# Spreading VectorE's dependent steps in the first pass of an attention and feed-forward kernel

## The chip, the cores and the metric

The kernel runs on one core of a Trainium2 chip. The metric is the device time of one execution in microseconds (us); less is better. The engines are called by the names of the profile: PE (TensorE, matrix products), DVE (VectorE), ACT (ScalarE), POOL (GpSimd) and SP (the engine that issues most DMAs).

## The reference

Chunked attention, then two feed-forward parts. What matters of it:

```python
def _attn_ref(q, k, v):              # 8 batches, 8 heads, 576 positions, 64 wide
    q_c, k_c, v_c = (t.reshape(B, H, 9, 64, 64) for t in (q, k, v))
    scores = 1 / sqrt(64) * matmul(q_c, k_c.transpose(0, 1, 2, 4, 3))
    scores = scores - max(scores, axis=-1, keepdims=True)
    attn = exp(scores)
    attn = attn / (sum(attn, axis=-1, keepdims=True) + 1e-09)
    return matmul(attn, v_c)

x = attn_out.transpose(0, 2, 1, 3).reshape(4608, 512)
h = x @ w_in                         # 512 -> 2048
x = (h * cos(h)) @ w_out             # 2048 -> 512
a, b = x @ w1, x @ w2                # 512 -> 1024 each
out = ((a * b) @ w3) @ w_out2        # 1024 -> 1024 -> 512
```

All of it is f32. The inputs q and k are scaled so that the softmax is not flat.

## The kernel before

**Products.** A product of f32 operands is made of three matmuls on operands split in a high and a low part (hi·hi, hi·lo, lo·hi: lines L111, L112, L113). So each activation and each weight has to be split: ACT or DVE writes the high part, DVE or POOL the low part by a subtraction. For the weights of the first feed-forward part this is done in the kernel: `conv_a`, `conv_b`, `conv_c` (called once each by `conv_tick`, for three different weight tiles in different stages) shift and mask the bits of a weight (L137, L138), add its low half (L144), and split the sum (L189 on ACT, L215 on DVE). From tile 1 on, the `st_...` functions do the same for the weights of later parts (L279, L280, L282, L310), and `sum_make`, `sum_hi`, `sum_lo` make sums of weight blocks for a scheme in which seven products stand for eight ("Seven"; `B11`, `T1` and the like are its operands, made by `x_op` and by L106/L107).

**Tiles.** The 4608 tokens go in 9 tiles of 512. A tile's tokens are four attention blocks of 128 tokens, 36 blocks in all. In the first pass the program goes through tiles 0 to 8, and in each through five groups of hidden columns of the first feed-forward part; a second pass does the other three groups, and then the last stage does the second feed-forward part. While a tile goes through its first four groups, the attention of one block of the next tile runs beside each; the fifth group has no attention, but makes the next tile's operands. Only the first four blocks (0 to 3) have nothing to run beside: they stand in front of tile 0.

**A block's attention** has these steps (the letters are those of the order below): A, scores (PE, L401), their maximum (DVE, L416 for blocks 0 to 3, L421 later) and its subtraction (DVE, L418 or L422); B, exp (ACT, L428); E, the sum (DVE, L433), + 1e-9 (L434), reciprocal (L436) and product (L437); C, four transposes (PE, L444) and a copy to SBUF (ACT, L447); D, the values (PE, L459), the scores of the next block (PE, L401) and a copy of the values into `xf` (ACT, L465 for blocks 0 to 3, L469 later).

**A group's work beside it:** the products of its hidden columns (in tiles 2 and up: `1`, `2`, `5`, `3` in the order, with seven products, and DVE's adds `d`, `e`, `d` between them at L549, L559, L561, L568), the range reduction of the cosine's argument (`a`, `c` on ACT at L607, `A`, `C` on DVE at L612), cos (`b`, `d`, ACT L617), the product with the cosine (`B`, `D`, DVE L621), the split of the result g (`s`: ACT L629, POOL L630 from tile 1 on), and the two halves (`x`, `y`) of the group before's product with w_out (`acc<-g,w`).

**The order** is written out by hand. Each engine takes its instructions in the order in which the program issues them, and waits at the first whose input isn't there. For blocks 0 to 3 it is the string `START`, for a tile's groups a string for the kind of tile: `ORDER0` (tile 0), `ORDER1P` (tile 1), `ORDER1` (tiles 2 to 7), and with an E at its end for the fifth group. A letter issues the part named above; `q` is the next step of attention, `v` a `conv_tick`, `x` in `START` a `conv_tick` too, `o` an operand of the seven products, `l`, `m`, `h`, `r` steps of `st_...`, `M`, `H`, `R` of `sum_...`. Buffers of the tile pools and PSUM banks add the waits that reuse needs.

Of the kernel before, what the change touches and what calls it, by code (L numbers as in the profile page):

```python
# [57 lines left out]
def chunk_attention_two_ffn(  # L58
# [42 lines left out]
    def f32(ap):  # L101
        return ap.bitcast(F32)
# [23 lines left out]
    def conv_a(key):  # L126
# [10 lines left out]
        nc.vector.tensor_scalar(m, hi, 3, 0x3FFFFFFF, op0=ALU.logical_shift_left, op1=ALU.bitwise_and)  # L137
        nc.vector.scalar_tensor_tensor(m, hi, 0xC0000000, m, op0=ALU.bitwise_and, op1=ALU.bitwise_or)  # L138
        halfway[key] = m

    def conv_b(key):

        m = halfway[key].bitcast(I32)
        nc.vector.tensor_tensor(out=m, in0=m, in1=raws.pop(key)[:, :, 0].bitcast(I32), op=ALU.add)  # L144
        if key[0] == "in":
            nc.sync.dma_start(out=wr[key[1] // 2][:, key[1] % 2], in_=m.bitcast(F32))
# [48 lines left out]
    def conv_tick():  # L195

        last = None
# [5 lines left out]
        if cat[2] < cat[1]:  # L203
            conv_b(cq[cat[2]])
            cat[2] += 1
        if cat[1] < cat[0]:
            conv_a(cq[cat[1]])
            cat[1] += 1
        if last:
# [4 lines left out]
            else:  # L214
                nc.vector.tensor_tensor(out=t[:, 1], in0=w, in1=f32(t[:, 0]), op=ALU.subtract)  # L215
# [13 lines left out]
    def sum_make():  # L229
# [10 lines left out]
        sp["parts"] = [(W[pair, 1][:, :, 0:256], s1), (w, spare[:, 0]), (new_s4((pair, 3)), s4)]  # L240

# [28 lines left out]

    def st_bits():
# [3 lines left out]
        key = now.pop("low")  # L275
        raw = raws.pop(key)
        lo, hi = raw[:, :, 0], raw[:, :, 1]
        m = wk.tile([P, TT], U32, tag="cw", name="cw", bufs=3)
        nc.vector.tensor_scalar(m, hi, 3, 0x3FFFFFFF, op0=ALU.logical_shift_left, op1=ALU.bitwise_and)  # L279
        nc.vector.scalar_tensor_tensor(m, hi, 0xC0000000, m, op0=ALU.bitwise_and, op1=ALU.bitwise_or)  # L280
# [113 lines left out]
    def att_scores_mm(j, early):  # L394
# [55 lines left out]
    def att_values(j, early):  # L450
# [908 lines left out]
```

## Time and profile before

| | us |
|---|---|
| time, median of 3 runs (lowest, highest) | 1453.41 (1452.62, 1454.89) |
| time of the profiled execution | 1455.09 |
| span of the profiled execution | 1453.3 |
| PE busy in the span | 1419.9 (98%) |
| DVE busy | 1200.6 (83%) |
| ACT busy | 717.5 (49%) |
| POOL busy | 202.2 (14%) |
| mean granted clock of PE | 0.998 of full speed |

"Busy" sums the durations of an engine's instructions. A row of a timeline gives start and duration in us, engine, line of the kernel before, operation, output and input by the program's names, shapes, a count where several equal instructions are put together, and in square brackets the idle time in front of it with what ended that. The waits are the idle times of one engine grouped by the line that waited and the instruction that it waited for.

### The profile page before, as it was taken

The numbers are of one execution on the slowest core, as the hardware profiler recorded it, in microseconds if no ns is written. First come the engines' busy times: TensorE is split into PE (matmuls) and PEld (weight loads), VectorE is DVE, ScalarE is ACT, GpSimd is POOL, SyncE is SP. The second block draws the span as 40 slices with busy tenths as digits, with TensorE's granted clock in tenths as the row PEclk, the third lists the DMA queues.
The fourth block names the chain that finished last, engine by engine and source line by source line (L and its number), as shares of the span: only waits on it lengthen the run. The fifth ranks groups of instructions, "written<-read, shape, count | busy, mean of one in ns | idle before, by whom it ended". The sixth has DMA issues, their size and how long they took to land.

```text
span 1453.3 us, 27397 instructions
## 1 busy us (share of the span) xinstructions
PE 1419.9 (98%) x10572; PEld 1260.6 (87%) x10572; DVE 1200.6 (83%) x1995; ACT 717.5 (49%) x1201; POOL 202.2 (14%) x151
## 2 busy tenths in 40 slices
PE   5899999999999999999999999999999999999998
PEld 5788878888888889888888889998898888889888
DVE  7989899899998987777777888776797888788787
ACT  4877677777777774444445544331132133123122
POOL 0112112222222222222212223020000000000000
PEclk9999999999999999999999999999999999999999
DMA  8866556566664628989899984697565765856643
GB/s 274 259 201 194 212 158 239 178 216 231 197 237 162 224 98 320 364 303 339 306 311 346 366 318 168 231 364 261 217 231 192 266 202 174 326 170 207 232 145 116
DMA packets 152481, 347.31 MB, mean 239 GB/s; under 512 B 15392, under 2 KB 53024, under 8 KB 151200
## 3 DMA queue, kind: packets, MB, share of 16 engines
q1 hardware_dynamic: 151200, 343.47, 68.2%
q0 software_dynamic: 1152, 2.10, 0.8%
q8 instruction: 84, 1.38, 0.4%
q14 instruction: 45, 0.37, 0.1%
HBM read 241.96 MB, written 101.45 MB: 236 GB/s over the span
## 4 chain that ended last, share of the span: by engine, by line
PE 59%; DMA 1%; DVE 1%; POOL 1%; ACT 1%; issue 0%; SPq 0%; POOLq 0%; ACTq 0%
PE ps_hh L111 7%; PE ps_hh L112 7%; PE ps_hh L113 7%; PE acc L112 7%; PE acc L113 7%; PE acc L111 7%; PE ps_aa L111 5%; PE ps_aa L112 5%; PE ps_aa L113 5%; POOL g L630 1%; DMA sd<-spare 0%; DMA raw<-in_w_dram 0%; DMA wfd<-wfo 0%; ACT T L106 0%; DVE x2a L659 0%
## 5 line engine op out<-in xcount | busy, mean ns | idle before, releaser
L630 POOL TENSOR_TENSOR g<-t,g 128x512 fp32r<-128x512 f32 x134 | 187.0, 1416 | 637.0 <-ACT g L629 596.7
L111 PE MATMUL acc<-g,w 128*128 128x512 f32 x576 | 228.1, 396 | 0.0
L112 PE MATMUL acc<-g,w 128*128 128x512 f32 x576 | 227.0, 394 | 0.4
L113 PE MATMUL acc<-g,w 128*128 128x512 f32 x576 | 225.0, 391 | 0.0
L860 ACT ACTIVATE phl<-w 128x512 fp32r<-128x512 f32 x66 | 41.3, 631 | 292.0 <-DVE w L1051 242.1
L113 PE MATMUL ps_hh<-T,w 128*128 128x256 f32 (+1 forms) x616 | 181.8, 295 | 1.7 <-DVE w L215 1.7
L111 PE MATMUL ps_hh<-T,w 128*128 128x256 f32 (+1 forms) x616 | 181.8, 295 | 0.0
L112 PE MATMUL ps_hh<-T,w 128*128 128x256 f32 (+1 forms) x616 | 181.6, 295 | 0.0
L112 PEld LDWEIGHTS acc<-g,w 128*128 128x128 f32 x576 | 108.5, 188 | 23.8 <-POOL g L630 4.0
L113 PEld LDWEIGHTS acc<-g,w 128*128 128x128 f32 x576 | 108.2, 188 | 22.8
L111 PEld LDWEIGHTS acc<-g,w 128*128 128x128 f32 x576 | 108.5, 188 | 19.6
L113 PEld LDWEIGHTS ps_hh<-T,w 128*128 128x128 f32 x616 | 118.2, 192 | 4.8 <-DVE w L215 2.3
L111 PE MATMUL ps_hh<-B,w 128*128 128x256 f32 (+1 forms) x396 | 120.2, 304 | 1.1 <-ACT xf L465 0.5
L111 PEld LDWEIGHTS ps_hh<-T,w 128*128 128x128 f32 x616 | 118.3, 192 | 2.7
L112 PEld LDWEIGHTS ps_hh<-T,w 128*128 128x128 f32 x616 | 118.3, 192 | 2.4
L112 PE MATMUL ps_hh<-B,w 128*128 128x256 f32 (+1 forms) x396 | 116.5, 294 | 0.0
L113 PE MATMUL ps_hh<-B,w 128*128 128x256 f32 (+1 forms) x396 | 116.3, 294 | 0.0
L617 ACT ACTIVATE t<-t,half_pi 128x512 f32<-128x512 f32 x144 | 98.5, 716 | 1.1
L629 ACT ACTIVATE g<-t 128x512 fp32r<-128x512 f32 x144 | 85.4, 628 | 12.3 <-DVE t L621 10.6
L607 ACT ACTIVATE t<-d 128x512 int32<-128x512 f32 x62 | 39.2, 632 | 103.3 <-DVE d L561 99.6
L111 PEld LDWEIGHTS ps_hh<-B,w 128*128 128x128 f32 x396 | 76.5, 193 | 6.6 <-PE acc L113 0.8
L549 DVE TENSOR_TENSOR d<-x,ps_hh 128x512 f32<-128x512 f32 x70 | 47.9, 685 | 40.5 <-ACT g L629 27.2
(304 smaller groups left out, 3775.5 us busy)
## 6 DMA issues: line engine op xcount, KB each, us to landing
w<-sd SPq DMA_DIRECT2D x159, 512.0 KB, 5.6
sd<-raw SPq DMA_DIRECT2D x104, 256.0 KB, 4.3
wset<-twd SPq DMA_DIRECT2D x26, 512.0 KB, 4.0
s<-sd SPq DMA_DIRECT2D x43, 256.0 KB, 5.7
wset<-wfd SPq DMA_DIRECT2D x42, 256.0 KB, 4.4
qk<-in_q_dram SPq DMA_DIRECT2D x36, 256.0 KB, 4.0
qk<-in_k_dram SPq DMA_DIRECT2D x36, 256.0 KB, 4.2
x2a<-x2o SPq DMA_DIRECT2D x36, 256.0 KB, 3.1
```

Source lines behind the costliest of these rows:

```text
L111: nc.tensor.matmul(ps, a[0], b[0], start=first, stop=False)
L112: nc.tensor.matmul(ps, a[0], b[1], start=False, stop=False)
L113: nc.tensor.matmul(ps, a[1], b[0], start=False, stop=last)
L549: nc.vector.tensor_tensor(out=two(self.d), in0=self.x1.unsqueeze(1).to_broadcast([P, 2, 256]), in1=two(p26), op=ALU.add)
L607: nc.scalar.activation(t.bitcast(I32), h, AF.Copy, scale=INV2PI, bias=0.25)
L617: nc.scalar.activation(t, t, AF.Sin, scale=TWO_PI, bias=half_pi)
L629: nc.scalar.activation(hi, r, AF.Copy)
L630: (nc.vector if i < GA else nc.gpsimd).tensor_tensor(out=lo, in0=r, in1=f32(hi), op=ALU.subtract)
L860: nc.scalar.activation(put[kind, f][0], plane(*SRC[kind], f), AF.Copy)
```

## The change

The text of `START` and of the orders changes, and with it the steps that an order can name. The attention's step A is cut in scores and maximum (A) and subtraction (F); step E in sum (E), + 1e-9 (G), reciprocal (I) and product (K). `conv_tick` issues DVE's instructions of its three stages in another order (shift, add, sign, low part; before: add, shift, sign, low part) and can issue attention steps between them. `st_bits` is cut in shift (`t`), sign (`n`) and the rest (`m`); `sum_make` in two parts (`M`, `N`). In `START` the scores of block 3 (`M3`) are issued before the transposes of block 0.

```diff
-START = "A0 A1 B0 x B1 E0 A2 C0 B2 E1 A3 D0 C1 x B3 D1 E2 o o E3 C2 D2 x C3 D3 x o o"
+START = "A0 F0 A1 F1 B0 x B1 E0 A2 M3 G0 I0 F2 K0 C0 B2 E1 A3 G1 I1 F3 K1 D0 C1 B3 x2 D1 o o x3 C2 D2 C3 D3 x o o"
-ORDER0 = "PsvaAqQvqcCqxybBdvDqvq"
+ORDER0 = "PsvaqAqQvqqcCqxybqBqdvDqvq"
-ORDER1P = "PsqMhQqqHaclAxbqCrRBmdyqDL"
+ORDER1P = "PsqMqNhQqqHaclAqtqxbCqnqrRBmdyqDL"
-ORDER1 = "1s2qMh5qqHa3clAxbqCrRmBdyqDL"
+ORDER1 = "1sq2qMNh5qqHa3cqlAqtqxbCnqrRmBdyqDL"
...
-        nc.vector.tensor_scalar(m, hi, 3, 0x3FFFFFFF, op0=ALU.logical_shift_left, op1=ALU.bitwise_and)
-        nc.vector.scalar_tensor_tensor(m, hi, 0xC0000000, m, op0=ALU.bitwise_and, op1=ALU.bitwise_or)
         halfway[key] = m
+        return (lambda: nc.vector.tensor_scalar(m, hi, 3, 0x3FFFFFFF, op0=ALU.logical_shift_left, op1=ALU.bitwise_and),
+                lambda: nc.vector.scalar_tensor_tensor(m, hi, 0xC0000000, m, op0=ALU.bitwise_and, op1=ALU.bitwise_or))
...
-    def conv_tick():
+    def conv_tick(between=()):
...
         if cat[2] < cat[1]:
-            conv_b(cq[cat[2]])
+            add = conv_b(cq[cat[2]])
             cat[2] += 1
         if cat[1] < cat[0]:
-            conv_a(cq[cat[1]])
+            bits = conv_a(cq[cat[1]])
             cat[1] += 1
+        ops = [*bits[:1], *([add] if add else ()), *bits[1:]]
...
-                nc.vector.tensor_tensor(out=t[:, 1], in0=w, in1=f32(t[:, 0]), op=ALU.subtract)
+                ops.append(lambda: nc.vector.tensor_tensor(out=t[:, 1], in0=w, in1=f32(t[:, 0]), op=ALU.subtract))
+        between = list(between)
+        for op in ops:
+            op()
+            if between:
+                between.pop(0)()
+        for op in between:
+            op()
...
+        nc.vector.tensor_tensor(out=s1, in0=a21, in1=a22, op=ALU.add)
+        sp["parts"] = None
+        yield
         nc.vector.tensor_tensor(out=s3, in0=a11, in1=a21, op=ALU.subtract)
-        nc.vector.tensor_tensor(out=s1, in0=a21, in1=a22, op=ALU.add)
         nc.vector.tensor_tensor(out=s2, in0=s1, in1=a11, op=ALU.subtract)
...
+    def att_sum(j, early):
+        sums[j] = sm = small.tile([P, 2 * HP], F32, tag="sm", name="sm")
+        nc.vector.reduce_sum(out=sm, in_=att[j], axis=AX.X)
+
+    def att_guard(j, early):
+        nc.vector.tensor_scalar_add(sums[j], sums[j], 1e-9)
+
+    def att_recip(j, early):
+        sm = sums[j]
+        sums[j] = rc = small.tile([P, 2 * HP], F32, tag="rc", name="rc")
+        nc.vector.reciprocal(rc, sm)
+
     def att_scale(j, early):
-        ex = att[j]
-        sm = small.tile([P, 2 * HP], F32, tag="sm", name="sm")
-        nc.vector.reduce_sum(out=sm, in_=ex, axis=AX.X)
-        nc.vector.tensor_scalar_add(sm, sm, 1e-9)
-        rc = small.tile([P, 2 * HP], F32, tag="rc", name="rc")
-        nc.vector.reciprocal(rc, sm)
+        ex, rc = att[j], sums.pop(j)
         nc.vector.tensor_tensor(
             out=ex, in0=ex, in1=rc.unsqueeze(2).to_broadcast([P, 2 * HP, 64]), op=ALU.mult)
...
-            if tok == "x":
-                conv_tick()
+            if tok[0] == "x":
+                conv_tick([lambda s=s_: att_tok(s + tok[1:], True) for s_ in "EGIK"] if tok[1:] else ())
...
-        steps = [s + str(j) for j in range(4, NJ) for s in "ABECD"]
+        steps = [s + str(j) for j in range(4, NJ) for s in "AFBEGIKCD"]
```

What this makes of VectorE's order is shown at three places. A row is the line, the operation, and output <- inputs with the columns.

First, the blocks in front of tile 0, with the buffers' numbers. `ex_260` belongs to block 1, `sm_312` and `rc_315` (after: `sm_330`, `rc_339`) are its sum and reciprocal; `mx_339` (after: `mx_335`) is block 3's maximum and `ps_s0`, `ps_s1` hold its scores. Before:

```order
L433 TENSOR_REDUCE sm_312<-ex_260 128x8
L434 TENSOR_SCALAR sm_312<-sm_312 128x8
L436 RECIPROCAL rc_315<-sm_312 128x8
L437 TENSOR_TENSOR ex_260<-ex_260,rc_315 128x512
L416 TENSOR_REDUCE mx_339<-ps_s0_318 128x4
L416 TENSOR_REDUCE mx_339<-ps_s1_319 128x4
L418 TENSOR_TENSOR two_301<-ps_s0_318,mx_339 128x4x64
L418 TENSOR_TENSOR two_301<-ps_s1_319,mx_339 128x4x64
```

After, at the same place:

```order
L466 TENSOR_REDUCE sm_330<-ex_260 128x8
L442 TENSOR_REDUCE mx_335<-ps_s0_300 128x4
L442 TENSOR_REDUCE mx_335<-ps_s1_301 128x4
L469 TENSOR_SCALAR sm_330<-sm_330 128x8
L474 RECIPROCAL rc_339<-sm_330 128x8
L451 TENSOR_TENSOR two_297<-ps_s0_300,mx_335 128x4x64
L451 TENSOR_TENSOR two_297<-ps_s1_301,mx_335 128x4x64
L478 TENSOR_TENSOR ex_260<-ex_260,rc_339 128x512
```

Block 1's product (L437, after L478), ahead of block 3's maximum before, now stands behind its maximum and its subtraction.

Second, the end of the same stretch on VectorE: block 3's sum and product, and the two low parts of operands (L107) ahead of them. Before:

```order
L107 TENSOR_TENSOR B11_176<-xf_174,B11_176 128x512
L107 TENSOR_TENSOR B21_177<-xf_174,B21_177 128x512
L433 TENSOR_REDUCE sm_408<-two_301 128x8
L434 TENSOR_SCALAR sm_408<-sm_408 128x8
L436 RECIPROCAL rc_411<-sm_408 128x8
L437 TENSOR_TENSOR two_301<-two_301,rc_411 128x512
L144 ISA cw_371<-raw_196,cw_371 128x1024
L137 TENSOR_SCALAR cw_443<-raw_270 128x512
L138 SCALAR_TENSOR_TENSOR cw_443<-raw_270,cw_443 128x512
L215 TENSOR_TENSOR w_439<-cw_266,w_439 128x512
```

After:

```order
L107 TENSOR_TENSOR B11_176<-xf_174,B11_176 128x512
L107 TENSOR_TENSOR B21_177<-xf_174,B21_177 128x512
L138 TENSOR_SCALAR cw_410<-raw_270 128x512
L466 TENSOR_REDUCE sm_413<-two_297 128x8
L146 ISA cw_370<-raw_196,cw_370 128x1024
L469 TENSOR_SCALAR sm_413<-sm_413 128x8
L139 SCALAR_TENSOR_TENSOR cw_410<-raw_270,cw_410 128x512
L474 RECIPROCAL rc_419<-sm_413 128x8
L220 TENSOR_TENSOR w_408<-cw_266,w_408 128x512
L478 TENSOR_TENSOR two_297<-two_297,rc_419 128x512
```

The four instructions of a weight conversion stood behind block 3's product and now stand between its steps, ahead of the product.

Third, a group of tiles 2 to 7 on VectorE, without buffers' numbers (`ps_at` is the bank of the attention, `ps_hh` the banks of the hidden columns, `t` the cosine's argument, `cw` a weight's bits). Before:

```order
L549 TENSOR_TENSOR d<-x_2503,ps_hh 128x512
L421 TENSOR_REDUCE mx<-ps_at 128x8
L422 TENSOR_TENSOR ex<-ps_at,mx 128x2x4x64
L559 TENSOR_TENSOR e<-d,ps_hh 128x512
L561 TENSOR_TENSOR d<-e,ps_hh 128x256
L433 TENSOR_REDUCE sm<-ex 128x8
L434 TENSOR_SCALAR sm<-sm 128x8
L436 RECIPROCAL rc<-sm 128x8
L437 TENSOR_TENSOR ex<-ex,rc 128x512
L568 TENSOR_TENSOR e<-e,ps_hh 128x512
L612 SCALAR_TENSOR_TENSOR t<-d,t 128x512
```

After:

```order
L444 TENSOR_REDUCE mx<-ps_at 128x8
L594 TENSOR_TENSOR d<-x_2503,ps_hh 128x512
L454 TENSOR_TENSOR ex<-ps_at,mx 128x2x4x64
L604 TENSOR_TENSOR e<-d,ps_hh 128x512
L606 TENSOR_TENSOR d<-e,ps_hh 128x256
L466 TENSOR_REDUCE sm<-ex 128x8
L613 TENSOR_TENSOR e<-e,ps_hh 128x512
L469 TENSOR_SCALAR sm<-sm 128x8
L657 SCALAR_TENSOR_TENSOR t<-d,t 128x512
L474 RECIPROCAL rc<-sm 128x8
L291 TENSOR_SCALAR cw<-raw 128x512
L478 TENSOR_TENSOR ex<-ex,rc 128x512
```

The maximum now stands ahead of the add that frees a bank of the hidden columns (L549, after L594), and between the sum and the product stand a 512-wide add, a step of the cosine and a shift of weight bits. On PE the order is the same but for one place: block 0's transposes stand behind block 3's scores. On SP and POOL nothing moves. On ACT, from tile 1 on, the copy of the transposes (L447, after L488) stands behind the load of the cosine's table and the first cosine, where before it stood ahead of both.

## Rows read from the trace of the kernel before

**Rows 1.** Busy time by stretch: start and end, length, each engine, clock, DMA.

```profile
0.00:100.00 100.00, 77.23 (x909) 68.21 (x910) 86.00 (x165) 71.40 (x120) 7.98 (x14) 0.97 0.85 258
...
200.00:545.00 345.00, 343.21 (x3355) 301.87 (x3355) 310.32 (x546) 262.05 (x416) 79.66 (x57) 1.00 0.58 194
545.00:1454.00 909.00, 903.29 (x5360) 805.27 (x5358) 715.45 (x1131) 310.42 (x547) 95.68 (x67) 1.00 0.73 259
```

**Rows 2.** Waits of PE for VectorE: total us, times, longest.

```profile
PE ps_at L444 <- DVE ex L437: 10.6, 7, 3.7
...
PE ps_hh L113 <- DVE w L215: 1.7, 3, 0.6
PE ps_hh L111 <- DVE d L549: 1.5, 2, 1.4
```

**Rows 3.** Timeline of PE, from the first blocks to the first group.

```profile
15.21 1.13 PE L401 MATMUL ps_s<-qk 64*64 64x64 f32 x32 [1.46 <-DMA qk<-in_k_dram]
...
17.13 1.12 PE L444 MATMUL ps_at<-ident,ex 128*128 128x128 f32 x4
...
28.32 0.58 PE L111 MATMUL ps_hh<-B,w 128*128 128x256 f32 x1 [0.47 <-ACT xf L465]
...
41.10 1.12 PE L444 MATMUL ps_at<-ident,ex 128*128 128x128 f32 x4 [3.67 <-DVE ex L437]
```

**Rows 4.** Timeline of VectorE in the first blocks.

```profile
16.39 0.76 DVE L416 TENSOR_REDUCE mx<-ps_s 128x4 f32<-128x256 f32 x2 [0.78 <-PE ps_s L401]
...
21.55 1.29 DVE L107 TENSOR_TENSOR B<-xf,B 128x512 fp32r<-128x512 f32 x2 [0.32 <-ACT B L106]
...
23.91 0.69 DVE L437 TENSOR_TENSOR two<-two,rc 128x512 f32<-128x512 f32 x1
...
25.13 0.42 DVE L137 TENSOR_SCALAR cw<-raw 128x512 uint32<-128x512 uint32 x1
```

**Rows 5.** Tile 1, a group with weight sums: VectorE, then PE.

```profile
119.95 0.69 DVE L437 TENSOR_TENSOR ex<-ex,rc 128x512 f32<-128x512 f32 x1
...
122.19 0.60 PE L444 MATMUL ps_at<-ident,ex 128*128 128x128 f32 x4
```

**Rows 6.** Tile 2, timeline of PE where an add comes late.

```profile
183.01 0.39 PE L111 MATMUL ps_hh<-B,s 128*128 128x256 f32 x1 [1.39 <-DVE d L549]
```

**Rows 7.** Tile 3, VectorE in a group that is not the tile's first.

```profile
268.99 0.69 DVE L549 TENSOR_TENSOR d<-x,ps_hh 128x512 f32<-128x512 f32 x1 [0.29 <-PE ps_hh L113]
...
270.32 0.69 DVE L422 TENSOR_TENSOR ex<-ps_at,mx 128x512 f32<-128x512 f32 x1
...
271.98 0.68 DVE L433 TENSOR_REDUCE sm<-ex 128x8 f32<-128x512 f32 x1
272.69 0.17 DVE L434 TENSOR_SCALAR sm<-sm 128x8 f32<-128x8 f32 x1
272.89 0.20 DVE L436 RECIPROCAL rc<-sm 128x8 f32<-128x8 f32 x1
273.13 0.69 DVE L437 TENSOR_TENSOR ex<-ex,rc 128x512 f32<-128x512 f32 x1
273.74 0.68 DVE L568 TENSOR_TENSOR e<-e,ps_hh 128x512 f32<-128x512 f32 x1
```

**Rows 8.** The same group: ACT, then PE.

```profile
271.20 0.63 ACT L428 ACTIVATE ex<-ex 128x512 f32<-128x512 f32 x1
...
276.21 1.28 ACT L617 ACT_TABLE_LOAD   x1
...
274.48 0.60 PE L444 MATMUL ps_at<-ident,ex 128*128 128x128 f32 x4
...
277.77 0.70 PE L459 MATMUL ps_at<-pt,vt 64*64 64x64 f32 x32
```

**Rows 9.** The first group of a later tile: VectorE, then PE.

```profile
292.62 0.68 DVE L549 TENSOR_TENSOR d<-x,ps_hh 128x512 f32<-128x512 f32 x1
...
293.36 0.39 PE L111 MATMUL ps_hh<-B,s 128*128 128x256 f32 x1
```

More of the change, by code (lines that the diff above doesn't have):

```diff
@@ L193, in chunk_attention_two_ffn @@
     cq, cat = [], [0, 0, 0, 0]
-    def conv_tick():
-        last = None
+    def conv_tick(between=()):
+        last, add, bits = None, None, ()
         if cat[3] < cat[2]:
@@ L269, in st_low, with st_shift, st_sign @@
             nc.scalar.activation(lo.bitcast(I32), lo, AF.Copy, scale=2.0 ** -29)
+    def st_shift():
+        if "low" in now:
+            now["m"] = m = wk.tile([P, TT], U32, tag="cw", name="cw", bufs=3)
+            hi = raws[now["low"]][:, :, 1]
+            nc.vector.tensor_scalar(m, hi, 3, 0x3FFFFFFF, op0=ALU.logical_shift_left, op1=ALU.bitwise_and)
+    def st_sign():
+        if "low" in now:
+            m = now["m"]
+            hi = raws[now["low"]][:, :, 1]
+            nc.vector.scalar_tensor_tensor(m, hi, 0xC0000000, m, op0=ALU.bitwise_and, op1=ALU.bitwise_or)
     def st_bits():
@@ L274, in st_bits @@
             return
-        key = now.pop("low")
+        key, m = now.pop("low"), now.pop("m")
         raw = raws.pop(key)
[L277 to L280, printed above, removed]
+        lo = raw[:, :, 0]
         mi = m.bitcast(I32)
@@ L407, in att_scores @@
             att_scores_mm(j, early)
+        while qk_at[0] < min(NJ, j + 2 + early):
+            load_qk(qk_at[0])
         ps = scores.pop(j)
@@ L416, in att_scores, with att_below @@
                 nc.vector.reduce_max(out=mx[:, c], in_=ps[c], axis=AX.X)
+        else:
+            nc.vector.reduce_max(out=mx, in_=ps, axis=AX.X)
+        scores[j] = ps, mx, ex
+    def att_below(j, early):
+        ps, mx, ex = scores.pop(j)
+        if early:
             for c in range(2):
@@ L473, in att_tok @@
     def att_tok(step, early):
-        (att_scores, att_softmax, att_scale, att_transpose, att_values)["ABECD".index(step[0])](int(step[1:]), early)
+        part = {"A": att_scores, "F": att_below, "B": att_softmax, "E": att_sum, "G": att_guard, "I": att_recip,
+                "K": att_scale, "C": att_transpose, "D": att_values, "M": att_scores_mm}[step[0]]
+        part(int(step[1:]), early)
     OPS = ("B11", "B21", "T2", "T1", "T3", "B22", "T4")
@@ L1130, in chunk_attention_two_ffn @@
         n_sums = 0
+        sums2 = []
         fq = 0
@@ L1189, in chunk_attention_two_ffn @@
                         n_sums += 1
-                elif op == "M":
-                    if loaded and i > GA + loaded[0][0]:
-                        sum_make()
+                elif op in "MN":
+                    if op == "N" and sums2:
+                        next(sums2.pop())
+                    elif op == "M" and loaded and i > GA + loaded[0][0]:
+                        sums2.append(sum_make())
+                        next(sums2[0])
                 elif op in "HR":
@@ L1197, in chunk_attention_two_ffn @@
                     st_low()
+                elif op == "t":
+                    st_shift()
+                elif op == "n":
+                    st_sign()
                 elif op == "m":
@@ L1215, in chunk_attention_two_ffn @@
                     if i < iA and nth < 4:
-                        att_tok(steps[20 * n + 5 * nth + n_q], False)
+                        att_tok(steps[36 * n + 9 * nth + n_q], False)
                     elif i >= iB + FOLD and fq < 4 * FB2:
```

24 lines of the change are left out of this document (13 added, 11 removed).

## The prediction

> **What bounds the kernel now.** The busy time by stretch comes first [rows 1]. After 545 us PE is busy for 903 of 909 us, and from 200 to 545 us, where the later tiles of the first pass run, for 343.2 of 345. VectorE is busy for 310 of those 345 us, but that alone is no cost: PE sets the pace, and what VectorE does counts only where PE waits for it. Only the first 100 us are open: PE 77 of 100. So the second view is PE's waits [rows 2]. For VectorE they come to little: 10.6 us at the transposes (seven waits, for the softmax product L437), 1.7 at weights (L215, three waits), 1.5 at the add L549. Of the 10.6, two waits of about 3.7 stand in the first 42 us, the second in tile 0's first group [rows 3]. That is all that a quicker VectorE can give back, some 14 us, and any step of VectorE that comes later than its slack is paid in full, since PE has nothing else to do. So the change is judged by one question at each place: when do the transposes' input (the product), the freed bank (the add), and the low part of a weight come, against the moment at which PE gets there.
>
> **What an opened pair is worth.** In a group of tile 3 [rows 7] the sum L433 starts at 271.98 and takes 0.68; the guard that needs it starts at 272.69, 0.03 after its end. Guard, reciprocal and product follow each 0.03 to 0.04 after the one before. But the add L568, which doesn't need the product in front of it, starts at 273.74, 0.08 before that product ends (273.13 + 0.69). So a step behind its own input pays 0.11 us more than one behind another's, and a 512-wide step costs 0.61 in a stream. A group opens about six such pairs (maximum to subtraction, sum to guard, guard to reciprocal, reciprocal to product, shift to sign, sign to add): 0.7 us of VectorE. For the guard and the reciprocal behind another instruction there is no row. Bounds: their present spacing, 0.20 and 0.24, and their durations less 0.08, 0.09 and 0.12 [rows 7]. I take 0.10 and 0.12, since the 0.08 is what the one independent pair there shows. A shift of weight bits, 0.42 long [rows 4], costs 0.34 by the same step.
>
> The Trainium skill, "VectorE: DVE Perf Modes", section "The DRAIN you can't avoid", speaks against this: an instruction starts when the pipe is empty, and eight copies with a semaphore after each took as long as eight with one after the last. By that an opened pair gives nothing. The 0.03 after against 0.08 before the end [rows 7] does not agree with it.
>
> **The blocks in front of tile 0: +3.4 us.** The two places in the order show it. Block 3's scores start at 15.21, when their keys arrive [rows 3], and nothing in the order of the loads moves, so issuing them earlier brings them no earlier. Before, block 1's product was done ahead of block 3's maximum at 16.39 [rows 4], and its transposes ran at 17.13 [rows 3]. Now that product stands behind that maximum and its subtraction: 16.39 + 0.67 (two halves of the maximum) + 0.2 (guard, reciprocal, adjacent) + 0.7 (two halves of the subtraction, taken as long as the maximum's) + 0.69 (itself) is about 18.7. Block 1's transposes start at about 18.75, 1.6 late; its values, their copy and the low parts L107 behind them go from 21.55 [rows 4] to about 23.2. Behind L107 (1.2) VectorE now has ahead of block 3's product: shift 0.34, sum 0.61, add 0.61, guard 0.10, sign 0.61, reciprocal 0.12, low part 0.61, together 4.2. It starts at about 27.4 instead of 23.91 [rows 4], 3.45 late. From that product to the first matmul of group 0 it is 28.32 - 23.91 = 4.41 (transposes, copy, values, copy; all in a row), so that matmul goes to about 31.8. Nothing later gives this back, since the rest runs at PE's pace. Block 0's transposes, now behind block 3's scores, cost nothing by themselves: its values stood behind those scores before too. Ends: +1.8, if only the second part is paid (the 4.2 less the old 2.4 ahead of the product), and +4.6, with small steps at their present spacing and ACT's copies late as well.
>
> **Tile 0: -1.35.** In its first group the transposes at 41.10 wait 3.67 for the product [rows 3], and VectorE is on that path. The product now has the cosine's product ahead of it, +0.61, less two or three opened pairs, 0.26: +0.35 (0 to +0.6). In the other groups VectorE sheds about 0.9 a group (softmax and four conversions), so the three waits for weights, 0.6 at most [rows 2], should go: -1.7 (-1.7 to 0).
>
> **Tile 1: +0.6.** In three groups with weight sums the product ends at 120.64 and the transposes start at 122.19 [rows 5]: slack 1.55. Now two steps of the cosine (0.6 each) and a shift (0.34) stand ahead of it, 1.54, less what the pairs give. I take 0.2 each, 0 to 0.5.
>
> **Tile 2: -0.8.** VectorE is behind for two groups; PE waits 1.39 for the add [rows 6], and most of the 3.2 us of waits at transposes outside the two long ones [rows 2] is here. Two groups' savings, 1.4, less 0.6 for the maximum that now stands ahead of the add. Ends: -2.7 (nearly all of it) and +0.5.
>
> **Tiles 3 to 7, the first group of each: +4.0.** The third place in the order shows why. The add L549 frees a bank; it starts at 292.62 straight behind VectorE's earlier work and ends at 293.30; PE's next product starts at 293.36 [rows 9]. The maximum now stands ahead of the add: 0.6, with no slack. The products behind it come late too; I add 0.2 at the transposes: 0.8 in each of five groups. Ends: 0.2 and 0.9 a group (1.0 to 4.5), the low one if VectorE gets there earlier.
>
> **Tiles 3 to 7, the other fifteen groups: +2.5.** Here VectorE waits 0.29 before the add [rows 7], so the maximum fits in front, and the subtraction moves from 270.32 to about 269.8. The exp can follow by some 0.25 only: it ends a stream of ACT (271.20, 0.19 after its input's end at 271.01 [rows 7, 8]). The sum then starts at about 271.55 instead of 271.98. Behind it, up to the product: sum 0.61, add 0.61, guard 0.10, cosine step 0.61, reciprocal 0.12, shift 0.34, that is 2.4 where it was 1.15. The product ends at about 274.65 instead of 273.82; the transposes start at 274.48 [rows 8]. So 0.15 to 0.2 is lost, in groups with an extra sum or shift 0.25: about 2.5 in all, ends 0 and 0.35 each (0 to 5.2).
>
> ACT's copy of the transposes now stands behind the table load of 1.28 and one cosine. The values that read it start at 277.77, 2.7 us after the transposes end at 275.08 [rows 8], and the load starts earlier, because the add L568 that releases the step ahead of it comes at 272.2 instead of 273.74 [rows 7]. I take nothing. Without that lead the copy would end at about 276.2 + 1.3 + 0.6 + 0.6 = 278.7, 0.9 late in each group.
>
> The second pass and the last stage keep PE's order and its pace [rows 1]: nothing.
>
> **Sum.** 3.4 + 0.35 - 1.7 + 0.6 - 0.8 + 4.0 + 2.5 = +8.35. It is made against the profiled execution (1455.09, of which 1453.3 is span); the median of the three runs is 1.7 lower. I put the difference on the median: 1453.41 + 8.4 = 1461.8.
>
> **Rivals.**
>
> Slower, but at the start only. VectorE arrives 0.6 or more ahead in each tile's first group and 0.2 ahead in the others, so the groups of tiles 3 to 7 lose nothing. For it: 0.7 saved a group. Against it: in [rows 9] the add is at the end of VectorE's queue. 3.4 + 0.35 - 1.7 + 0.6 - 0.8 is +1.85: 1455.3.
>
> Faster. VectorE's saved time reaches PE: the 1.7, the 3.2 at transposes and the 1.4 at the add go, -6.3, and the start loses its lower end, +1.8: -4.5, 1448.9. Its place is tiles 0 to 2; it decides if the keys of block 3 come some 1.4 us before 15.21, so that block 1's product isn't late, and if VectorE keeps 0.6 of slack in tiles 3 to 7. For it: these waits are real. Against it: the loads keep their order.
>
> An opened pair gives nothing, as a mechanism of this kernel: the small steps keep 0.20, 0.24 and 0.45. Then the start is +3.75, the product in fifteen groups 0.33 later (+5), the 1.7 stays and tile 2 gains nothing: about +16, 1469. The add at 273.74 [rows 7] speaks against it. The rule of "VectorE: DVE Perf Modes" named above would have it so.
>
> **How the numbers follow.** Chances: my sum 0.57, the start only 0.23, faster 0.14, pairs worth nothing 0.06. A measurement of this kernel tells about 0.2% from no change, 2.9 us: 1450.5 to 1456.3. The start-only case lies mostly within it (0.17), the low edge of my sum too (0.03). Faster 0.14, same 0.20, slower 0.66. The lower ends together make about -1.6, the upper ones +17, but they won't all fall on one side; the range leaves out the faster case and the worthless pairs: 1453.5 to 1467.5.
>
> **What would show it.** In the trace after: the first matmul of group 0 near 31.8, behind a product of block 3 at 27.4; in each tile's first group PE waiting some 0.6 for the add (now L594); waits of 0.1 to 0.4 at the transposes for the product (L478) in tiles 3 to 7; no waits at the weights (L220); small steps 0.09 to 0.13 apart from the next. I am wrong if the first matmul starts before 30, if the add in a first group starts no later against PE than before, or if the table load of the cosine makes the values wait for their copy.

## The result, and the profile after

The changed kernel takes 1464.51 us (median of four runs, 1463.69 to 1465.79) against 1453.01 (four runs of the kernel before). The ratio is 1.0077, with a 95% interval of 1.0063 to 1.0091: slower by about 11.2 us. The prediction was 1461.8, in a range of 1453.5 to 1467.5.

Busy time by stretch, as in [rows 1] (start and end, length, then PE, PE's weight loads, VectorE, ACT, POOL, PE's clock, DMA share, GB/s), of the changed kernel:

```profile
0.00:100.00 100.00, 74.19 (x895) 65.32 (x896) 79.37 (x160) 69.00 (x116) 7.79 (x14) 0.97 0.81 247
...
200.00:545.00 345.00, 338.67 (x3330) 296.20 (x3329) 292.42 (x538) 260.69 (x412) 78.26 (x57) 1.00 0.57 192
```

VectorE's busy time from 200 to 545 us fell from 310 to 292 us. Part of that is work that now falls behind 545 us. Between the same two events, the first transposes of blocks 15 and 35, it is 273.7 us (485 instructions) before and 262.3 (484) after: the spread steps do save some 11 us of its time. PE's busy time fell too, from 343.2 to 338.7, since it now waits more. PE's waits of the changed kernel, as in [rows 2]:

```profile
PE ps_at L485 <- DVE ex L478: 10.6, 9, 4.0
PE ps_hh L111 <- DVE d L594: 3.7, 5, 0.7
PE ps_v L500 <- ACT two L488: 3.1, 2, 2.4
PE ps_at L500 <- ACT pt L488: 2.7, 4, 0.7
...
PE ps_hh L113 <- DVE w L220: 1.5, 3, 0.5
```

The transposes wait as long as before (10.6), at other places; the add waits 3.7 instead of 1.5, in five places; the weights still wait 1.5.

Where the time went is best read from one event that every kernel has, the first transpose of each attention block on PE. The table gives its start in each profile and how much later it is than in the kernel before; negative is earlier. Blocks 4 to 7 run in tile 0, 8 to 11 in tile 1, and so on, and blocks 12, 16, 20, 24, 28 and 32 in the first group of a tile.

| block | before, us | after, us | later by | softmax and start of before, only the weights spread (experiment 5): later by |
|---|---|---|---|---|
| 3 | 24.66 | 27.86 | 3.20 | -0.12 |
| 4 | 41.10 | 44.47 | 3.37 | -0.92 |
| 8 | 109.20 | 112.40 | 3.20 | -1.97 |
| 11 | 148.16 | 152.76 | 4.60 | -1.97 |
| 12 | 173.18 | 178.42 | 5.24 | -2.09 |
| 13 | 188.79 | 192.82 | 4.03 | -3.44 |
| 14 | 201.21 | 206.80 | 5.59 | -3.56 |
| 15 | 213.48 | 219.18 | 5.70 | -3.57 |
| 16 | 236.81 | 243.22 | 6.41 | -3.58 |
| 35 | 516.57 | 527.55 | 10.98 | -5.39 |

So the start costs about 3.2, tile 0 nothing, tile 1 1.4, block 14 a step of 1.56 that no wait there explains (below), each tile's first group about 0.7, and the rest a tenth or two at a time; tile 2 gives 0.57 back (block 11 to 13). The last column is the experiment that came out faster than both; it stands here to be read beside the others.

In the first blocks (timeline of PE, changed kernel; compare [rows 3]):

```profile
14.57 1.25 PE L427 MATMUL ps_s<-qk 64*64 64x64 f32 x32 [5.46 <-DMA qk<-in_k_dram]
15.76 1.11 PE L485 MATMUL ps_at<-ident,ex 128*128 128x128 f32 x4
17.56 1.14 PE L500 MATMUL ps_v<-ex,vt 64*64 64x64 f32 x32 [0.69 <-ACT ex L488]
18.62 1.11 PE L485 MATMUL ps_at<-ident,ex 128*128 128x128 f32 x4
...
31.36 0.58 PE L111 MATMUL ps_hh<-B,w 128*128 128x256 f32 x1 [0.47 <-ACT xf L506]
```

and on VectorE there (compare [rows 4]; the second line is block 1's product, the last block 3's):

```profile
15.86 0.76 DVE L442 TENSOR_REDUCE mx<-ps_s 128x4 f32<-128x256 f32 x2 [2.26 <-PE ps_s L427]
...
17.46 0.68 DVE L478 TENSOR_TENSOR ex<-ex,rc 128x512 f32<-128x512 f32 x1
...
27.12 0.68 DVE L478 TENSOR_TENSOR two<-two,rc 128x512 f32<-128x512 f32 x1
```

Block 3's product starts at 27.12 (27.4 was forecast; 23.91 before), the first matmul at 31.36 (31.8; 28.32 before). PE waited 5.46 us for block 3's keys, which now stand ahead of block 0's transposes.

A tile's first group, VectorE and then PE (compare [rows 9]):

```profile
299.34 0.68 DVE L444 TENSOR_REDUCE mx<-ps_at 128x8 f32<-128x512 f32 x1
299.94 0.68 DVE L594 TENSOR_TENSOR d<-x,ps_hh 128x512 f32<-128x512 f32 x1
...
300.67 0.39 PE L111 MATMUL ps_hh<-B,s 128*128 128x256 f32 x1 [0.74 <-DVE d L594]
```

The maximum takes the place that the add had, and PE waits 0.74. This is there in the first group of each of tiles 3 to 7.

A later group, VectorE, then PE (compare [rows 7] and the last but one of [rows 8]):

```profile
278.15 0.68 DVE L466 TENSOR_REDUCE sm<-ex 128x8 f32<-128x512 f32 x1
278.74 0.68 DVE L613 TENSOR_TENSOR e<-e,ps_hh 128x512 f32<-128x512 f32 x1
279.34 0.16 DVE L469 TENSOR_SCALAR sm<-sm 128x8 f32<-128x8 f32 x1
279.41 0.68 DVE L657 SCALAR_TENSOR_TENSOR t<-d,t 128x512 f32<-128x512 f32 x1
280.01 0.19 DVE L474 RECIPROCAL rc<-sm 128x8 f32<-128x8 f32 x1
280.13 0.37 DVE L291 TENSOR_SCALAR cw<-raw 128x512 uint32<-128x512 uint32 x1
280.42 0.68 DVE L478 TENSOR_TENSOR ex<-ex,rc 128x512 f32<-128x512 f32 x1
...
281.15 0.66 PE L485 MATMUL ps_at<-ident,ex 128*128 128x128 f32 x4
```

From the sum's start to the product's start it is 2.27 us, where it was 1.15. Each step starts about 0.08 before the one in front of it ends, the guard (the step that adds 1e-9) costs 0.07, the reciprocal 0.12: VectorE loses no time between steps, and the product comes later, as other work stands in its chain.

### The profile page after: what moved, and what is told of

Its sections match the earlier page's. It is cut to its first block, busy times and chain, and to the rows that moved or that the text cites. A ratio compares the mean times of both kernels' runs of the same rounds, so it can differ in the third digit from the quotient of the medians.

```text
span 1463.4 us, 27436 instructions
## 1 busy us (share of the span) xinstructions
PE 1422.0 (97%) x10572; PEld 1259.6 (86%) x10572; DVE 1175.3 (80%) x1995; ACT 716.8 (49%) x1201; POOL 202.2 (14%) x151
## 3 DMA queue, kind: packets, MB, share of 16 engines
q1 hardware_dynamic: 151200, 343.47, 67.7%
## 4 chain that ended last, share of the span: by engine, by line
PE 60%; POOL 1%; ACT 1%; DVE 1%; issue 0%; POOLq 0%; ACTq 0%
PE ps_hh L111 8%; PE ps_hh L112 8%; PE ps_hh L113 8%; PE acc L112 7%; PE acc L113 7%; PE acc L111 7%; PE ps_aa L111 6%; PE ps_aa L112 6%; PE ps_aa L113 6%; POOL g L675 1%; ACT T L106 0%; DVE T L107 0%; ACT g L674 0%; ACT t L662 0%; ACT B L106 0%
## 5 line engine op out<-in xcount | busy, mean ns | idle before, releaser
L594 DVE TENSOR_TENSOR d<-x,ps_hh 128x512 f32<-128x512 f32 x70 | 47.9, 684 | 57.0 <-ACT g L674 50.0
```

The lines of the kernel that those rows point to most:

```text
L594: nc.vector.tensor_tensor(out=two(self.d), in0=self.x1.unsqueeze(1).to_broadcast([P, 2, 256]), in1=two(p26), op=ALU.add)
```

## The experiments

All kernels are compared with the kernel before on the same chip. "Lateness" is the number of the table: the start of a block's first transpose against the kernel before.

**1. The start put back.** The order ahead of tile 0 as before, all else as changed.

```diff
-START = "A0 F0 A1 F1 B0 x B1 E0 A2 M3 G0 I0 F2 K0 C0 B2 E1 A3 G1 I1 F3 K1 D0 C1 B3 x2 D1 o o x3 C2 D2 C3 D3 x o o"
+START = "A0 F0 A1 F1 B0 x B1 E0 G0 I0 K0 A2 F2 C0 B2 E1 G1 I1 K1 A3 F3 D0 C1 x B3 D1 E2 G2 I2 K2 o o E3 G3 I3 K3 C2 D2 x C3 D3 x o o"
```

> The changed kernel, with the stretch ahead of tile 0 in the order of before (block 3's scores behind block 0's transposes, each block's sum, guard, reciprocal and product in a row, weights converted behind block 3's product). Theory: that stretch costs what it moves, the trace of after has its first matmul at 31.36 against 28.32, and block 4's transposes 3.4 us late; so the first matmul comes back to about 28.3 and the time falls by about 3.2, to 1461.3. Rival: the wait of 4.05 at the transposes of the first group, which VectorE sets, swallows it, since VectorE then has the conversions still to do: the time falls by less than 1 us, 1464.

Measured: 1461.11 us, before 1454.44, ratio 1.0045 (1.0030 to 1.0060). The first matmul starts at 28.35, and block 4 is 0.82 early where it was 3.37 late: the start's cost is real and is not swallowed. From block 14 to 35 the lateness grows by 5.4 as in the changed kernel. At block 14 the step of 1.56 is missing here.

**2. The maximum behind the add again**, in tiles 2 to 7.

```diff
-ORDER1 = "1sq2qMNh5qqHa3cqlAqtqxbCnqrRmBdyqDL"
+ORDER1 = "1s2qqMNh5qqHa3cqlAqtqxbCnqrRmBdyqDL"
```

> The changed kernel, with the maximum behind the add again in tiles 2 to 7 (maximum and subtraction in a row). Theory: the five waits of 0.74 for the add in the first group of tiles 3 to 7 go, 3.7 us, and 0.1 comes back per group where the subtraction follows its own maximum but has slack: about -3.5, 1461. Rival: VectorE's queue is as late with the add in front, because the maximum only changes places with other work, and the wait moves to the transposes of the same group: less than 1.5 us.

Measured: 1472.97 us, ratio 1.0126 (1.0110 to 1.0141): 8.5 more than the changed kernel's median, 7 by the two ratios. Both expectations fell. PE's waits:

```profile
PE ps_at L485 <- DVE ex L478: 20.5, 28, 4.0
```

The waits for the add are gone, but the transposes now wait for the product in 28 places. Each group of tiles 3 to 7 now adds about 0.6 of lateness, where the changed kernel adds 0.1 in most. So the maximum ahead of the add, which costs the first groups 0.7, pays for a part of what the other moves cost everywhere else: in blocks 16 to 35 the exp starts 1.76 us behind the first add (L594) in the changed kernel and 2.05 here, the sum 2.44 and 2.98 (medians).

**3. Sum to product in a row**, ahead of the last add, with the maximum still ahead; here the transposes also stand behind `b`, as in the changed kernel.

```diff
-ORDER1 = "1sq2qMNh5qqHa3cqlAqtqxbCnqrRmBdyqDL"
+ORDER1 = "1sq2qMNh5qqqqqHa3clAtxbqCnrRmBdyqDL"
```

> The changed kernel, with sum, guard, reciprocal and product in a row ahead of the last add in tiles 2 to 7; the maximum still ahead of the first add. Theory: what stands between the sum and the product makes the transposes late; the waits of 0.74 (three) fall to 0.3 or less, tile 2's 1.56 and 1.95 fall by 0.6 each, and the 0.1 lost in each other group goes: -1.7 for tiles 3 to 7, -1.2 for tile 2, and with the wait of 1.95 shortened the clock of 0.57 behind it is not seen, another -1.5: 1460 to 1461.5. Rival: the transposes wait for the exp on ACT, and the order of what follows it matters little: within 1 us of the changed kernel.

Measured: 1463.36 us, ratio 1.0060 (1.0043 to 1.0076): 1.2 less than the changed kernel's median, 2.5 by the two ratios, so between the rival and the theory. PE's waits:

```profile
PE ps_at L500 <- ACT pt L488: 8.2, 14, 1.0
PE ps_at L485 <- DVE ex L478: 6.2, 6, 4.0
```

The waits at the transposes fell as the theory has it (4.0 of the 6.2 us is the first group), but new ones stand in their place: the values wait for ACT's copy. Four of the 14 places, 2.7 us, are tile 0's and are there before too; the ten others, 5.5 us, are in tiles 2 to 7. The last add is behind the product again, and with it the table load that the copy stands behind.

**4. Only the weights' part**, with the transposes behind `b`.

```diff
+START = "A0 F0 A1 F1 B0 x B1 E0 G0 I0 K0 A2 F2 C0 B2 E1 G1 I1 K1 A3 F3 D0 C1 x B3 D1 E2 G2 I2 K2 o o E3 G3 I3 K3 C2 D2 x C3 D3 x o o"
+ORDER0 = "PsvaAqqQvqcCqqqqxybBdvDqvq"
+ORDER1P = "PsqqMNhQqqqqqHaclAtxbqCnrRBmdyqDL"
+ORDER1 = "1s2qqMNh5qqqqqHa3clAtxbqCnrRmBdyqDL"
```

> Only the weights' part of the change: conversions (shift, add, sign, low part), the bits' steps and the sums spread as in the changed kernel; all of the softmax and the stretch ahead of tile 0 as before. Theory: VectorE has less to do, but PE waits for it no less, since in tile 0 the order that leads to the late weight starts at an exp and a cosine of ACT: 1452 to 1454, within 1 us of before. Rival 1: the weights' order alone costs what after lost outside the first blocks, 6 us or more. Rival 2: it is worth the 1.7 us of waits at weights and more: 1450 or less.

Measured: 1465.61 us, ratio 1.0078 (1.0062 to 1.0093). Taken alone that looks like rival 1. The waits say what it is:

```profile
PE ps_at L500 <- ACT pt L488: 19.0, 28, 1.0
```

Four of the 28, 2.7 us, are tile 0's, as before; the other 24, 0.5 to 1.0 us each, are in tiles 2 to 7. This kernel kept one thing of the softmax's change: ACT's copy of the transposes behind the cosine's table load, where before has it ahead in these tiles (in tile 1 it stands behind the load before too, from 123.33 us behind a load from 121.40, and no wait comes of it). ACT in one group, then PE, then the copy in the kernel before, whose table load follows at 276.21 [rows 8]:

```profile
277.03 0.63 ACT L652 ACTIVATE t<-e 128x512 int32<-128x512 f32 x1 [1.73 <-DVE e L613]
...
278.24 1.28 ACT L662 ACT_TABLE_LOAD   x1
279.54 0.73 ACT L662 ACTIVATE t<-t,half_pi 128x512 f32<-128x512 f32 x1
280.17 0.58 ACT L488 ACTIVATE pt<-ps_at 128x512 f32<-128x512 f32 x1
...
280.80 0.69 PE L500 MATMUL ps_at<-pt,vt 64*64 64x64 f32 x32 [0.54 <-ACT pt L488]
```

```profile
275.61 0.58 ACT L447 ACTIVATE pt<-ps_at 128x512 f32<-128x512 f32 x1
```

The last add is late as before, ACT's step that waits for it (1.73) holds the table load, and the copy ends at 280.75. In the changed kernel that add stands ahead of the product, so the table load starts before the transposes and the copy costs nothing.

**5. The same with the copy ahead of the table load**, as before has it in tiles 2 to 7 (here in tile 1 too).

```diff
-ORDER1P = "PsqqMNhQqqqqqHaclAtxbqCnrRBmdyqDL"
-ORDER1 = "1s2qqMNh5qqqqqHa3clAtxbqCnrRmBdyqDL"
+ORDER1P = "PsqqMNhQqqqqqHaclAtxqbCnrRBmdyqDL"
+ORDER1 = "1s2qqMNh5qqqqqHa3clAtxqbCnrRmBdyqDL"
```

> As the kernel with only the weights' part of the change, but with the copy of the transposes ahead of the cosine's table load on ACT, as before has it (there it stood behind the table load and the first cosine, and PE waited for it at 28 places, 19.0 us in all). Theory: those waits, about 0.7 each in tiles 1 to 7, go; the weights' part alone is then no loss: 1452 to 1454 on a chip where before takes 1453 to 1454. Rival: the copy's waits turn into waits for the product: 1460 or more.

Measured: 1449.89 us, before 1453.57, ratio 0.9972 (0.9962 to 0.9982): faster than both kernels by more than was expected. Busy time and the waits that are left:

```profile
200.00:545.00 345.00, 343.94 (x3369) 303.57 (x3368) 306.57 (x547) 262.13 (x418) 81.25 (x58) 1.00 0.58 196
```

```profile
PE ps_at L485 <- DVE ex L478: 9.8, 4, 4.0
...
PE ps_hh L113 <- DVE w L220: 0.9, 3, 0.4
...
PE ps_hh L111 <- DVE d L594: 0.5, 2, 0.3
```

The gain stands in tile 0 (1.05 from block 4 to 8, with the weights' waits down to 0.9), in tile 2 (1.47 from block 11 to 13: the late add [rows 6] is in time) and at three groups with an extra sum in tiles 3 to 5 (0.6 each). The copy's place in tile 1 does nothing: from block 8 to 11 the lateness stands still in experiments 4 and 5 alike. So the weights' half of the change is worth 4 to 5 us, and the softmax's half, the copy's new place among it, and the start cost some 15 to 16.

**6 and 7. The two parts of the start.** One puts block 3's sum to product back ahead of the conversion; the other puts its scores back behind block 0's transposes, with block 1's product ahead of its maximum.

```diff
-... B3 x2 D1 o o x3 C2 D2 C3 D3 x o o
+... B3 x2 D1 o o E3 G3 I3 K3 C2 D2 x C3 D3 x o o
```

> The changed kernel, with block 3's sum, guard, reciprocal and product in a row behind the two low parts (L107), ahead of the conversion's four instructions. Theory: four conversion instructions stand ahead of that product in the changed kernel; here it starts about 1.8 us earlier (25.3 against 27.12), the transposes follow at once, and the first matmul comes at about 29.7 instead of 31.36: -1.6, 1463. Rival: the copy of block 2's transposes on ACT, which came 2.43 late there, holds the last values up just as long: no change.

```diff
-... A2 M3 G0 I0 F2 K0 C0 B2 E1 A3 G1 I1 F3 K1 D0 C1 B3 ...
+... A2 G0 I0 F2 K0 C0 B2 E1 G1 I1 K1 A3 F3 D0 C1 B3 ...
```

> The changed kernel, with block 3's scores behind block 0's transposes again and block 1's product ahead of block 3's maximum; the conversion still ahead of block 3's product. Theory: block 0's transposes come at about 13 instead of 15.76, block 1's at 17.2 instead of 18.62, the low parts (L107) at 21.6 instead of 23.04, the first matmul at about 30 instead of 31.36: -1.4. With the part that the kernel with block 3's product first measures, the two should add up to the 3.0 of the whole stretch. Rival: block 3's product is bound by what stands ahead of it on VectorE, whatever the early blocks do: no change.

Measured: 1463.75 us (ratio 1.0065, 1.0050 to 1.0080) and 1462.96 (1.0062, 1.0047 to 1.0077). Block 3's keys land at another time in each execution (the scores start at 13.85 to 16.75 over all kernels here), so the first matmul is counted from those scores: before 28.32 - 15.21 = 13.1, changed 31.36 - 14.57 = 16.8, with the product first 30.32 - 15.25 = 15.1, with the scores back 28.52 - 13.85 = 14.7. The two parts are worth 1.7 and 2.1, together 3.8 against 3.7 of the whole, so both theories hold. With the scores back they start when block 0's transposes end, not at a landing, so the 2.1 may hold some of the keys' luck. The times of the two kernels also hold different stretches at PE's lower clock (last section), so the parts are read from the traces.

**8. The first group's softmax ahead of the conversion**, on the kernel before, for the very first group alone.

```diff
-ORDER0 = "PsvaAqQvqcCqxybBdvDqvq"
+ORDER00 = "PsvaqqAQqvcCxybBdvDqvq"
```

> The kernel before, with the very first group's order changed: the softmax of block 4 ahead of the weight conversion and of the cosine's second step, so that the product stands some 3 us earlier on VectorE. Theory: the wait of 3.67 at the transposes of that group falls below 1.2, and the half clock that shows behind it (0.80, 0.50 and 0.85 in the three stretches of 4 us from 38 to 50) goes or shortens; conversions that come later give back 1 us at most: -2.5 to -5, 1448 to 1451 against a before of 1453. Rival: VectorE is full through tile 0, and the conversions put off make weights late: within 1 us of before.

Measured: 1454.78 us, ratio 1.0010 (1.0000 to 1.0020): no gain. PE, then ACT:

```profile
36.86 0.66 PE L445 MATMUL ps_at<-ident,ex 128*128 128x128 f32 x4 [1.29 <-DVE ex L438]
42.05 1.13 PE L460 MATMUL ps_at<-pt,vt 64*64 64x64 f32 x32 [4.53 <-ACT pt L448]
```

```profile
39.71 0.72 ACT L618 ACTIVATE t<-t,half_pi 128x512 f32<-128x512 f32 x1 [1.22 <-DVE t L613]
...
41.41 0.59 ACT L448 ACTIVATE pt<-ps_at 128x512 f32<-128x512 f32 x1
```

The transposes are 4.2 early, and their copy stands behind a cosine that VectorE now feeds late. The lower clock of that group did not shorten either: it lasts 6.8 us, as before.

**9 and 10. The same on the weights' part, with the copy ahead of the conversion too; and the sums of weights behind the last add.**

```diff
+ORDER00 = "PsvaqqqAQqqqqqvcCxybBdvDvq"
-ORDER1 = "1s2qqMNh5qqqqqHa3clAtxqbCnrRmBdyqDL"
+ORDER1 = "1s2qqh5qqqqqa3cMNHlAtxqbCnrRmBdyqDL"
```

> The weights' part with the copy first (1449.9 where before takes 1453.6), and in the very first group the softmax of block 4 ahead of the conversion, with the transposes and their copy on ACT ahead of the conversion too (when only the softmax went ahead, the transposes came 4.2 us earlier and the values then waited 4.5 us for that copy). Theory: the wait of 3.5 at the transposes of the first group falls to about 1 and none at the values takes its place; conversions put off make weights late by 1 us at most: -1.5 to -3, 1447 to 1448.5. Rival: VectorE is full through tile 0, and what the first group gains is waited for at weights in the second: within 1 us of 1449.9.

> The same, and the sums of weight blocks in tile 2 behind the last add instead of ahead of the exp's sum. Theory: the two waits of 0.84 and 1.45 at the transposes of tile 2 go, -1.5 to -2.3 more against the kernel without it. Rival: the sums' splits come late and the group that uses them waits: no gain.

Measured: 1450.87 us (ratio 0.9979, 0.9970 to 0.9989) and 1450.64 (0.9980, 0.9971 to 0.9990): no better than 1449.89. In the first, block 4 is 3.3 earlier than in experiment 5 (1.0 of that is an earlier first matmul), and block 5 is 1.6 later: its next group waits for weights,

```profile
42.98 0.58 PE L112 MATMUL ps_hh<-B,w 128*128 128x256 f32 x1 [2.85 <-ACT w L194]
44.72 0.58 PE L114 MATMUL ps_hh<-B,w 128*128 128x256 f32 x1 [0.94 <-DVE w L221]
```

as the rival has it; PE's lower clock, which lasts 10.2 us there and 6.8 in experiment 5, takes a part too. In the second, both waits at tile 2's transposes (0.83 and 1.45) go, as the theory has it, but waits for ACT come in their place (0.87 for a copy out of a bank of the hidden columns, 0.23 and 0.49 for copies of transposes), and by block 14 some 0.6 is left.

**11. The weights' part and the maximum ahead of the add**, nothing else of the softmax.

```diff
-ORDER1 = "1s2qqMNh5qqqqqHa3clAtxqbCnrRmBdyqDL"
+ORDER1 = "1sq2qMNh5qqqqqHa3clAtxqbCnrRmBdyqDL"
```

> The weights' part with the copy first, and one part of the softmax's change alone: in tiles 2 to 7 the maximum ahead of the first add. Theory: the add of each first group of tiles 3 to 7 is 0.6 to 0.74 late, as in the changed kernel, and nothing pays for it, since the other groups' transposes hardly wait: +3 to +3.5, 1453 to 1453.5. Rival: with 0.7 us less work a group VectorE reaches the maximum early enough, and the wait for the add is under 0.2: within 1 us of 1449.9.

Measured: 1450.74 us (ratio 0.9979, 0.9970 to 0.9989). PE's waits for the add:

```profile
PE ps_hh L111 <- DVE d L594: 4.1, 6, 0.8
```

Five of them are 0.75, in the first groups of tiles 3 to 7: the mechanism is the theory's. The time is the rival's, within 1 us. The lateness grows by 0.45 at each of the five. But the two waits at tile 2's transposes are shorter (0.46 and 0.99 against 0.84 and 1.45), and this profile's start was 0.8 earlier than that of experiment 5. From block 13 to 35 it loses 1.6 against experiment 5.

**The maximum and the chain behind the sum together.** Change of lateness from block 13 to 35, tiles 2 to 7, from seven profiles:

| | maximum behind the add | maximum ahead |
|---|---|---|
| sum to product in a row, copy ahead of the table load | -1.95 (exp. 5) | -0.37 (exp. 11) |
| sum to product in a row, copy behind the load | +13.58 (exp. 4) | +6.06 (exp. 3) |
| sum to product spread over the group, copy behind the load | +13.51 (exp. 2) | +5.36 (exp. 1), +6.95 (changed) |

Alone the maximum's move costs 1.6; with the copy behind the load it saves 7.5 to 8, whether the chain is spread or not. The copy's move alone costs 15.5 with the maximum behind and 6.4 with it ahead. Spreading the chain on top of that costs nothing (-0.1 and -0.7): in the medians of blocks 16 to 35 with the maximum ahead, the product starts 1.1 us later behind the first add (4.71 in place of 3.60), but the last add 1.65 earlier (2.56 in place of 4.21), and with it the table load and the copy behind it (6.96 in place of 8.14). PE then waits for the product and no longer for the copy. What the spread chain would cost with the copy ahead of the load no run shows. The changed kernel's 6.95 holds the step at block 14, which experiment 1 has not.

## Why the prediction was right, point by point

**What bounds the kernel** held: VectorE lost work, PE lost time. **An opened pair** (two dependent steps with another instruction put between) held: 0.08 before the end in place of 0.03 after it; the guard was taken at 0.10 and costs 0.07, the reciprocal 0.12 as taken. Over blocks 15 to 35 the 11 us are 0.57 in each of 20 groups, where 0.7 was taken. So the rival of pairs worth nothing fell. The Trainium skill, "VectorE: DVE Perf Modes", section "The DRAIN you can't avoid", says that the next instruction doesn't start until the pipe is empty; its first paragraph excepts a next instruction that is not held, which starts earlier. The prediction left that exception out, and the rows above agree with it.

**The start, +3.4:** 3.04 at the first matmul, 3.20 at block 3. Counted from block 3's scores, which started 0.64 earlier in this execution, it is 3.7; that the number came so close to 3.4 is partly luck. The second half is as worked out. In the first half a step was wrong: "block 0's transposes, now behind block 3's scores, cost nothing by themselves". They made block 0's values late (17.56 against 16.09; the row of before is below), block 1's transposes stand behind those, and so start at 18.62, though their product was ready at 18.14. The product's delay alone would have made 1.0 of the 1.5; two causes of nearly one size lay on top of each other, and the sum was right by that. Block 0's values before:

```profile
16.09 1.10 PE L459 MATMUL ps_v<-ex,vt 64*64 64x64 f32 x32
```

**Tile 0:** the first group came as forecast (+0.35; the wait grew from 3.67 to 4.05). The -1.7 did not come: the weights still wait 1.5. The step that failed is "In the other groups VectorE sheds about 0.9 a group (softmax and four conversions), so the three waits for weights, 0.6 at most [rows 2], should go". From block 4 to 8 its busy time fell from 61.1 to 59.3 us, some 0.5 a group, and that did not reach the weights. VectorE in a group of tile 0, changed kernel:

```profile
56.38 0.69 DVE L466 TENSOR_REDUCE sm<-ex 128x8 f32<-128x512 f32 x1 [0.73 <-ACT ex L460]
...
58.91 0.69 DVE L666 TENSOR_TENSOR t<-t,ps_hh 128x512 f32<-128x512 f32 x1 [0.93 <-ACT t L662]
59.52 0.68 DVE L478 TENSOR_TENSOR ex<-ex,rc 128x512 f32<-128x512 f32 x1
```

What was saved is idle time at the exp and at the cosine, 1.66 us here, where the same group has 0.31 before (at 53.69, waiting for ACT): in the new order the work that used to fill it stands behind the instruction that waits. Experiments 1 and 5 differ in tile 0 by the softmax's order alone: from block 4 to 8 the one loses 0.36, the other gains 1.05. The other profiles with as long a stretch at the lower clock agree: 67.7 to 68.5 us with the softmax spread (changed, 1, 2, 3), 67.1 to 67.2 with it in a row (4, 5, 11), 68.1 before. Experiments 6 and 7, spread too, have that stretch 3.4 us shorter and longer and take 67.2 and 69.0.

**Tile 1, +0.6:** 1.40 (three groups of 0.46). The slack was right, but the first of the cosine's steps that stand ahead of the product waits 0.89 for ACT, which a sum of durations leaves out:

```profile
123.43 0.69 DVE L657 SCALAR_TENSOR_TENSOR t<-ps_hh,t 128x512 f32<-128x512 f32 x1 [0.89 <-ACT t L652]
```

**Tile 2, -0.8:** from block 11 to 13 -0.57, as forecast in sum: the wait of 1.39 for the add is gone, those at the transposes are 1.56 and 1.95 in place of 0.96 and 1.34.

**Tiles 3 to 7, first groups, +4.0:** 0.71, 0.74, 0.75, 0.71 and 0.73 in lateness, together 3.64. **The other groups, +2.5:** 10.98 - 5.59 - 3.64 = 1.75, of which 0.12 is tile 2's last block. **ACT's copy, nothing:** held, by the lead that the prediction named: in tiles 0 to 7 PE waits for it in tile 0 alone, as before. Experiments 3 and 4 show its price without the lead (0.9 forecast; waits of 0.5 to 1.0 in experiment 4). What was said of ACT's order, that the copy stood ahead of the table load before from tile 1 on, is wrong for tile 1, where it stood behind the load before too; no term of the sum hangs on that.

The forecast sum was 8.35, the traces give 10.98 up to block 35. The 2.6 between them is 1.5 of tile 0 (0.16 from the first matmul to block 8, where -1.35 was forecast), 0.8 of tile 1, 0.2 of tile 2 and 1.56 of a clock that fell (below), less 0.4 of the start and 1.1 of tiles 3 to 7. So the mechanism was right in the main in the start and in tiles 2 to 7, missed a wait in tile 1 and was wrong in tile 0, and errors of both signs made the sum. Behind block 35 the two profiles come 0.9 closer (spans 1463.4 and 1453.3), where nothing was forecast; no run here asks why. What the experiments add is that tile 0's gain was there to be had, with the weights spread and the softmax left alone.

## What to carry to other kernels

An instruction put between two dependent steps fills a gap of 0.1 us and pushes what follows by its whole length; on a chain that another engine waits for, spread only what that chain doesn't need. The start shows it (1.7 us for block 3's chain, experiment 6), and tile 0; in tiles 2 to 7 the runs do not part it from the copy's place. Ask of each instruction set in such a place what it waits for itself: here idle time at the exp and the cosine ate what the pairs gave. And a step moved on one engine may take a copy on another past a table load: separate such parts before judging either, as experiments 4 and 5 did.

## What was not expected of the hardware

After a wait of PE of nearly 2 us at block 13, its granted clock fell to the lower of its two levels (1.2 of 2.4 GHz) for some 3.4 us, in some executions and not in others. PE and then the stretch behind it (clock is the third number from the right), changed kernel:

```profile
192.82 0.66 PE L485 MATMUL ps_at<-ident,ex 128*128 128x128 f32 x4 [1.95 <-DVE ex L478]
193.23 0.56 PE L111 MATMUL acc<-g,w 128*128 128x512 f32 x1
193.59 0.63 PE L112 MATMUL acc<-g,w 128*128 128x512 f32 x1
```

```profile
193.00:197.00 4.00, 4.00 (x14) 3.18 (x14) 4.00 (x9) 2.49 (x4) 0.00 (x0) 0.57 0.40 100
```

and the same place with the scores put back (experiment 7):

```profile
190.35 0.66 PE L485 MATMUL ps_at<-ident,ex 128*128 128x128 f32 x4 [1.96 <-DVE ex L478]
...
191.07 0.39 PE L112 MATMUL acc<-g,w 128*128 128x512 f32 x1
```

```profile
190.50:194.50 4.00, 4.00 (x69) 3.23 (x72) 4.00 (x9) 2.52 (x4) 0.00 (x0) 1.00 0.36 121
```

A product of 512 columns takes 0.63 instead of 0.39 there, and PE loses 1.56 us beyond the wait. Of six waits of 1.93 to 1.96 at blocks 12 and 13 in five profiles, three were followed by the fall; none of the shorter ones at these blocks was. What tells the six apart stays open. Around tile 0's first group, where PE waits for up to 4 us, every profile shows the lower level, for 6.8 us in most, 3.4 in experiment 6 and 10.2 in experiments 7, 9 and 10; set beside the other profiles, that moves tile 0 by about 1 us (tile 0 above). The changed kernel's four runs have mean clocks of 0.996, 0.997, 0.997 and 0.996 and times of 1465.29, 1463.72, 1463.69 and 1465.79, which would fit a fall in two of the four (a longer stretch in tile 0 would fit as well); only the first has a trace.
